# A fused Fourier-filter and ReGLU kernel: another order for its opening, and one copy at its end

## The chip, the core and the metric

One core of one Trainium2 chip runs the whole program. The metric is the device time of one execution in microseconds (us), lower is better. The profile's engines are PE (TensorE: matmuls; PEld is its weight load), DVE (VectorE), ACT (ScalarE), POOL (GpSimd) and SP (SyncE, which here only issues DMAs). Each engine works through its own instructions in program order, and waits at an instruction until its inputs are there and its output buffer is free. DMAs are issued from SP, ACT and POOL; those of POOL are the only ones here that change the type (fp32 in HBM to bf16 on chip).

## The reference

```python
# x: (8, 3008, 256) fp32, filt_r and filt_i: (1505, 256)
X = np.fft.rfft(x, axis=1)
Y = X * (filt_r + 1j * filt_i)[None]
y = np.fft.irfft(Y, n=3008, axis=1).astype(np.float32)
# then a gated feed-forward layer on the 24064 rows of y
gate = np.maximum(y @ w_gate, 0.0)          # w_gate, w_val: 256 x 1536
out = ((gate * (y @ w_val)) @ w_out)        # w_out: 1536 x 256, fp32 out
```

## The kernel before, in words

The transform of length 3008 is split as 94 x 32. A sequence is handled in four stages: a first transform over the 94 rows (matrix `WA`, tiles `psA`, L265), a second one over the 32 columns (`fwd`, `psX`, L402), the product with the filters (`product`, L419 to L422), the inverse of the second transform (`inv`, `psD`, L445), and the inverse of the first (`item_c`, `psY`, L538), which gives 512 rows of y at a time, transposed, in `yT`. The feed-forward layer then runs over 47 blocks of 512 rows (`gv`, L555 to L560; `o_part`, L576 to L600). It is the long loop of the kernel. The stages of the sequences ("batches") 1 to 7 are put into that loop at fixed steps, so that they run amid the matmuls of the layer.

The change touches the opening, ahead of the loop, and the very end.

**The opening.** Batch 0 goes through all stages, and batch 1 through the first one. The order is written out by hand; the scheduler changes nothing of it.

- SP and ACT issue the loads of batch 0's x (`load_x`, L190), SP then the tables. POOL issues the two filters (`load_filters`): each is loaded in four pieces of odd rows (L231, read backwards) and four pieces of even rows (L236). The order is: odd pieces of the real filter, odd of the imaginary, even of the real, even of the imaginary. POOL's DMAs share eight semaphores in turn, so a DMA waits until the one eight before it has landed.
- A one-line DMA on SP, `hold` (L647), reads two rows of the real filter `Ftr` and so waits for its first odd and first even piece. Behind it SP issues batch 1's x, in four quarters of three DMAs each (256 KB per DMA), into the buffers that batch 0's x had.
- PE makes the first transform of batch 0 (`a_0`), ACT copies the tiles out (L277), DVE transposes four quarters (`turn_0`, L300).
- `first_b`: `fwd(0, i)` for i = 0 to 5, each into two PSUM banks (e = 0, 1). For each bank there are two products, k = 0 with the real filter (`tt`) and k = 1 with the imaginary (`uu`). Those of (i, e) = (0, 1), (1, 1), (2, 1) go by way of an ACT copy (`xs`, L419) to POOL (L420), all others are DVE's (L422). `make_back_u` makes a table on ACT (L216, L218) that `inv` needs. `inv(0, q)`, q = 0 to 2, takes the products of i = 2q and 2q + 1, fills four banks, and is copied out to `DS0` (L458). `warm(n)` runs n matmuls on junk (L611).
- Amid this stand the "items": batch 1's first transform in 16 pieces (`a_1`), each one `psA` bank and one ACT copy (L290; half of them in two parts). Items 0 to 3 need the first quarter of batch 1's x, 4 to 7 the second, and so on. When item 13 is done, SP stores a half of the result to HBM and loads it back in another layout.
- After the third inverse, DVE turns `DS0` in two halves of d (`turn_d`, L300), `item_c(0, 0)` and `item_c(0, 1)` make the first `yT`, and the loop starts with its first `psV`.

There are eight PSUM banks. A stage takes the one that was given back longest ago and waits until whoever read it last is done. Before the change two, two and two items stand in `first_b`, then come seven, the two `item_c`, and the last three.

**The end.** The last block's output is copied bank by bank (L589) and stored from three DMA queues (L600). The last of its four tiles is copied in two halves: columns 0 to 127 by DVE (L585), columns 128 to 255 by ACT (L586).

Of the kernel before, what the change touches and what calls it, by code (L numbers as in the profile page):

```python
# [116 lines left out]
def kernel(  # L117
# [18 lines left out]
    W = 512  # L136
# [19 lines left out]
    def done(t):  # L156
        free.append(held.pop(id(t))[0])
# [68 lines left out]
    def load_filters():  # L226

        for src, dst in FILT:
            for c in range(4):
                r, k1, n = 32 * c + 1, 1 + H * c, H - c // 3  # L230
                nc.gpsimd.dma_start(dst[r:r + 31:2, :n, :],  # L231
                                    _ap(src, (N1 - k1) * D, [[N1 * D, 16], [-D, n], [1, D]]))
        for src, dst in FILT:
            for c in range(4):
                r, k1, n = 32 * c, 1 + H * c, H - c // 3
                nc.gpsimd.dma_start(dst[r:r + 31:2, :n, :], _ap(src, k1 * D, [[N1 * D, 16], [1, n * D]]))  # L236
# [31 lines left out]
    def a_0(n2, nn, d0, nd):  # L268

        psA = a_bank(n2, nn, d0, nd)  # L270
        dq = D // 4
        l, q = n2 % NC2, slice(d0 // dq, (d0 + nd) // dq)
        c = n2 // NC2
        dst = AS0.rearrange("p q (l c) e (g f) -> p l c g q e f", c=2, g=2)[:, l:l + nn, c // 2, c % 2]
        src = psA.rearrange("p n (q e f) -> p n q e f", e=dq // 2, f=2)
        for i in range(nd // dq):
            nc.scalar.copy(dst[:, :, q.start + i], src[:, :, i])  # L277
        done(psA)

    def a_1(p, s, h):  # L280
# [21 lines left out]

    def turn_0(q):
        w = D // 8
        turn_pairs(ats[0][:, :, q * w:q * w + w], AS0[:, q])

    def turn_1(i):
        w = D // 8
# [79 lines left out]
    ON_POOL = ((0, 1), (1, 1), (2, 1))  # L388
    ats = {}

    psXs, tus, left, xs = {}, {}, {}, {}
# [43 lines left out]
    def inv(b, q):  # L435
# [3 lines left out]
        for m in range(2):  # L439
            for k in range(last + 1):  # L440
                for r in range(2):
                    for c in range(4):
                        for e in range(2):
# [6 lines left out]
        dst = sb.tile([128, 8, D], BF16, tag="dsb", bufs=3, name="dsb") if b else DS0  # L450
        def out(cs):
            for c in cs:
                copy = nc.vector.tensor_copy if (c % 2 if b else (q, c) in ((1, 3), (2, 0), (2, 1))) else nc.scalar.copy
                if b:
                    copy(dst[:, c:8:4, :], psD[c])
                else:
                    k, g = 4 * q + c // 2, c % 2 * 2
                    copy(dst[:, k:k + 3:2, :, g:g + 2], psD[c].rearrange("p m (f e) -> p m e f", f=2))  # L458
                done(psD[c])
        if not b:  # L460
            return out(range(4))

        def rest():
            out((2, 3))
# [6 lines left out]

    def first_b(item):

        def products(i, es=(1, 0)):
            for e in es:
                for k in range(2):
                    product(0, i, e, k, pool=(i, e) in ON_POOL)

        for i in range(3):
            fwd(0, i)  # L480
            if i < 2:
                products(i)
        make_back_u()
        products(2)
        warm(3)
        fwd(0, 3)
        products(3, (1,))
        warm(3)
        fwd(0, 4)
        item(2)  # L490
        products(3, (0,))
        inv(0, 0)
        fwd(0, 5)
        products(4)
        item(2)
        products(5)
        place_own()
        inv(0, 1)
        item(2)
        inv(0, 2)  # L500

    dCs = {}
# [29 lines left out]
    def item_c(k, h):  # L532

        if h == 0:
            yTs[k] = sb.tile([128, 2, W], BF16, tag="yT", bufs=3, name="yT")
        psY = bank("psY", W)
        for (o, b, n2, n1, w) in runs(k * W, W):
            nc.tensor.matmul(psY[:, o:o + w],  # L538
                             d_rows(b, n2, h),
                             M1[:, 1, n1:n1 + w] if b == 0 else M1[:NROW, 0, n1:n1 + w],  # L540
                             start=True, stop=True)
        dst = yTs[k][:, h]
        if h == 0 or k:
            nc.scalar.copy(dst, psY)  # L544
        else:
            nc.vector.tensor_copy(dst, psY)
        done(psY)


# [18 lines left out]
    def o_part(blk, s, prods):  # L568
# [9 lines left out]
        if s in (5, 11) or last and s % 3 == 2:  # L578
# [2 lines left out]
                osb = XP[t][:, 0:1, :].rearrange("p k (h d) -> p (k h) d", d=D)  # L581
            else:
                osb = fs.tile([128, 2, D], FP32, tag="osb", bufs=4)
            if s == 11 and last:
                nc.vector.tensor_copy(osb[:, 1, 0:D // 2], psO[:, 1, 0:D // 2])  # L585
                nc.scalar.copy(osb[:, 1, D // 2:], psO[:, 1, D // 2:])  # L586
            else:
                copy = nc.vector.tensor_copy if last else nc.scalar.copy
                copy(osb[:, t0 % 2:t % 2 + 1], psO[:, t0 % 2:t % 2 + 1])  # L589
            done(psO)  # L590
            late = last or blk == NB - 2 and s == 11
            for tt in range(t0, t + 1):
# [49 lines left out]
    for r in range(2):  # L642
        make_back_t(r)
        if not r:
            warm(4)
    hold = sb.tile([2, 8], BF16, tag="hold", bufs=1)
    nc.sync.dma_start(hold, Ftr[0:2, 4, 0:8])  # L647
    load_x(1, sp, ((0, 0, 2 * q), (0, 2 * q, 4 * q), (1, 0, 2 * q), (1, 2 * q, 4 * q)))
    items = iter([(p, s, h) for p in range(4) for h in range(2) for s in range(2)])

    def item(n):
# [110 lines left out]
```

## Time and profile before

| What | us |
|---|---|
| Median of 3 runs (866.09 to 868.73) | 868.37 |
| Time of the profiled execution | 865.68 |
| Its span, first to last instruction | 863.80 |
| Granted TensorE clock, mean | 0.999 |
| First matmul of the long loop (`psV`), from the span's start | 45.59 |
| Last matmul of the kernel ends | 858.21 |

The page's busy shares are: PE 98%, PEld 58%, DVE 67%, ACT 57%, POOL 53% of the span. A view of windows gives PE 4.09 us of 5 between 20 and 25 us and 4.59 of 5 between 25 and 30, part of it junk matmuls; it gives 5.00, 5.00 and 4.95 in the three windows of 5 us that follow 35. In the timeline a row gives the start and the time of a run of like instructions, the engine, the line, the operation, the tile written and read, the shape and the count; the bracket at its end says how long the engine had been idle before it and whose event ended that.

### The profile page before, as it was taken

To read this page: it belongs to the slowest core of one execution; us is meant where nothing else is said; L and a number is where in the kernel's file an instruction comes from. 1 tells how busy PE (TensorE), PEld (TensorE's weight loads), DVE (VectorE), ACT (ScalarE), POOL (GpSimd) and SP (SyncE) were. 2 spreads that over 40 slices of the span, in tenths; PEclk is the share of its full clock that TensorE was granted. 3 is DMA by queue.
4 is the path that set the end of the run, shared out by engine and by line. 5 is a ranking of instruction groups with operands and counts; after the bars stand their busy time and mean duration, and the time that the engine had idled before them with its cause. 6 is when DMAs were issued, how large, how long until landed. Compare 5 with 4: busy or idle time off the path is not lost.

```text
span 863.8 us, 20396 instructions
## 1 busy us (share of the span) xinstructions
PE 848.7 (98%) x7587; PEld 498.8 (58%) x7704; DVE 577.8 (67%) x863; ACT 494.6 (57%) x904; POOL 458.4 (53%) x496
## 2 busy tenths in 40 slices
PE   9999999999999999999999999999999999999997
PEld 4456655656556555556556655565655656666665
DVE  3878865777657775577765787658865688555553
ACT  5765565555655556555555555555556555555552
POOL 6747890488986765776666756767450023000001
PEclk9999999999999999999999999999999999999999
DMA  9985365334782339633386333762464422611111
GB/s 250 241 164 122 96 158 138 109 113 110 190 183 88 84 87 192 166 98 98 85 208 142 95 103 100 190 151 74 101 130 108 99 58 52 126 43 29 37 35 52
DMA packets 101366, 101.61 MB, mean 118 GB/s; under 512 B 21827, under 2 KB 89955, under 8 KB 99730
## 3 DMA queue, kind: packets, MB, share of 16 engines
q1 hardware_dynamic: 81986, 77.96, 36.1%
q0 software_dynamic: 18928, 21.82, 11.7%
q8 instruction: 61, 1.00, 0.5%
q10 hardware_dynamic: 352, 0.52, 0.2%
q14 instruction: 39, 0.32, 0.1%
HBM read 58.23 MB, written 45.88 MB: 121 GB/s over the span
## 4 chain that ended last, share of the span: by engine, by line
PE 94%; DMA 2%; issue 1%; DVE 1%; ACT 1%; SPq 1%; POOL 0%; DVEq 0%; ACTq 0%
PE psG L555 29%; PE psO L576 28%; PE psV L555 26%; PE psA L265 3%; PE psF L367 3%; PE psY L538 3%; PE psD L445 2%; PE psX L402 1%; DMA XF<-in_x_dram 1%; DMA Abuf<-asb 1%; ACT vsb L558 1%; DVE prod L560 1%; SPq L190 0%; DVE tt L422 0%; DMA out_dram<-osb 0%
## 5 line engine op out<-in xcount | busy, mean ns | idle before, releaser
L560 DVE SCALAR_TENSOR_TENSOR prod<-psG,vsb 128x512 bf16<-128x512 f32 x564 | 389.4, 691 | 235.8 <-ACT vsb L558 231.6
L558 ACT CAST vsb<-psV 128x512 bf16<-128x512 f32 x564 | 332.2, 589 | 225.8 <-PE psV L555 121.1
L576 PE MATMUL psO<-WoT,prod 128*128 128x256 bf16 x2256 | 336.6, 273 | 0.8
L555 PE MATMUL psG<-yT,WgT 128*128 128x512 bf16 x1111 | 331.8, 379 | 5.2
L555 PE MATMUL psV<-yT,WvT 128*128 128x512 bf16 x1030 | 314.9, 380 | 0.1
L576 PEld LDWEIGHTS <-prod 128*128 128x128 bf16 x2256 | 220.6, 98 | 143.4
L555 PEld LDWEIGHTS <-WgT 128*128 128x128 bf16 x1128 | 110.0, 97 | 133.5
L432 POOL TENSOR_TENSOR pp<-tt,uu 128x256 bf16<-128x256 f32 x84 | 60.9, 725 | 170.7 <-DVE uu L422 162.5
L555 PEld LDWEIGHTS <-WvT 128*128 128x128 bf16 x1128 | 100.3, 98 | 37.3 <-issue 25.6
L544 ACT CAST yT<-psY 128x512 bf16<-128x512 f32 x93 | 54.5, 586 | 43.2 <-PE psY L538 42.6
L589 ACT COPY osb<-psO 128x512 f32<-128x512 f32 x92 | 54.1, 588 | 22.1 <-PE psO L576 20.7
L600 POOL DMA_DIRECT2D out_dram<-osb x5 | 2.6, 534 | 119.6 <-ACT osb L589 118.0
L422 DVE TENSOR_TENSOR tt<-psX,Ftr 128x512 f32<-128x512 f32 (+1 forms) x93 | 63.5, 683 | 0.5 <-PE psX L402 0.5
L422 DVE TENSOR_TENSOR uu<-psX,Fti 128x512 f32<-128x512 f32 (+1 forms) x93 | 63.3, 681 | 0.3 <-DMA Fti<-in_filt_i_dram 0.3
L433 POOL TENSOR_TENSOR pp<-tt,uu 128x256 bf16<-128x256 f32 x84 | 60.9, 726 | 0.0
L353 POOL TENSOR_TENSOR fold<-XF 128x1024 f32<-128x1024 f32 x24 | 56.3, 2347 | 5.8 <-DMA XF<-in_x_dram 5.4
L354 POOL TENSOR_TENSOR XF<-XF 128x1024 f32<-128x1024 f32 x24 | 56.4, 2350 | 1.9
L257 POOL CAST scr<-prod 128x8 f32<-128x8 bf16 x19 | 3.6, 190 | 85.8 <-DVE prod L560 71.7
L340 POOL DMA_DIRECT2D XF<-in_x_dram x76 | 45.6, 602 | 2.0 <-issue 1.3
L374 ACT CAST asb<-psF 128x512 bf16<-128x512 f32 x48 | 25.8, 589 | 34.5 <-PE psF L367 34.5
L374 DVE CAST asb<-psF 128x512 bf16<-128x512 f32 x48 | 30.9, 686 | 18.0 <-PE psF L367 18.0
L538 PE MATMUL psY<-M,dCb 96*128 96x94 bf16 (+19 forms) x604 | 37.9, 200 | 0.0
(71 smaller groups left out, 457.8 us busy)
## 6 DMA issues: line engine op xcount, KB each, us to landing
Dbuf<-dsb SPq DMA_DIRECT2D x84, 128.0 KB
dCb<-Dbuf SPq DMA_DIRECT2D x56, 192.0 KB
XF<-in_x_dram POOLq DMA_DIRECT2D x38, 256.0 KB, 6.7
Abuf<-asb SPq DMA_DIRECT2D x96, 96.0 KB
at<-Abuf SPq DMA_DIRECT2D x24, 384.0 KB
XF<-in_x_dram SPq DMA_DIRECT2D x31, 256.0 KB
XF<-in_x_dram POOLq DMA_DIRECT2D x76, 96.0 KB, 5.1
out_dram<-osb SPq DMA_DIRECT2D x69, 94.0 KB
```

The lines of the kernel that those rows point to most:

```text
L353: tt(t, xp[:, 0:2], xp[:, 2:4], op=ALU.add)
L354: tt(xp[:, 2:4], xp[:, 0:2], xp[:, 2:4], op=ALU.subtract)
L374: copy(asf[:, :, q, :], banks[q])
L422: nc.vector.tensor_tensor(p, psX, filt, op=ALU.mult)
L432: nc.gpsimd.tensor_tensor(p[:, 0], tt[:, 0], uu[:, 1], op=ALU.subtract)
L433: nc.gpsimd.tensor_tensor(p[:, 1], tt[:, 1], uu[:, 0], op=ALU.add)
L538: nc.tensor.matmul(psY[:, o:o + w], d_rows(b, n2, h), M1[:, 1, n1:n1 + w] if b == 0 else M1[:NROW, 0, n1:n1 + w], start=True, stop=True)
L544: nc.scalar.copy(dst, psY)
L555: nc.tensor.matmul(pt[:, :W], w[:, h, ft * 128:(ft + 1) * 128], yt[:, h, :], start=(h == 0), stop=(h == 1))
L558: nc.scalar.copy(vsb, psV[:, :W])
L560: nc.vector.scalar_tensor_tensor(prod, in0=psG[:, :W], scalar=0.0, in1=vsb, op0=ALU.max, op1=ALU.mult)
L576: nc.tensor.matmul(psO[:, t % 2], prods[ft][:, t * 128:(t + 1) * 128], WoT[:, ft, :], start=(ft == 0), stop=(ft == NFT - 1))
```

## The change

- Filters: all eight pieces of the real one first, then all eight of the imaginary one.
- SP now has two `hold` DMAs. The first waits for the real filter's first odd and even pieces; behind it the first quarter of batch 1's x is issued. The second waits for the same pieces of the imaginary filter; behind it come the other three quarters.
- The last `a_0` tile is copied in two halves on ACT, and the last quarter of `turn_0` is transposed in two halves.
- `first_b`: `fwd` 0 to 3 stand together; then the real products, then items and imaginary products in turn. `make_back_u` stands behind the first two items. The two `warm(3)` are gone. Items now stand as 2, 2, 1, 2, 1 in `first_b`, then seven, the two `item_c`, and one.
- The copies out of `inv`: for q = 0 and 1 all four on ACT. For q = 2 by halves of d: the first half two on ACT and two on DVE, then `turn_d(0)`, the second half four on ACT, then `turn_d(1)`.
- `item_c(0, h)`: the left half of `yT` is copied by ACT, the right half by DVE.
- The end: the last tile is copied whole, by DVE.

```diff
@@ load_filters
                 nc.gpsimd.dma_start(dst[r:r + 31:2, :n, :],
                                     _ap(src, (N1 - k1) * D, [[N1 * D, 16], [-D, n], [1, D]]))
-        for src, dst in FILT:
             for c in range(4):
@@ a_0
-            nc.scalar.copy(dst[:, :, q.start + i], src[:, :, i])
+            for e in (slice(0, 16), slice(16, 32)) if (n2, d0) == (24, 3 * dq) else (slice(0, 32),):
+                nc.scalar.copy(dst[:, :, q.start + i, e], src[:, :, i, e])
@@ turn_0
-        turn_pairs(ats[0][:, :, q * w:q * w + w], AS0[:, q])
+        n = 2 if q == 3 else 1
+        for i in range(n):
+            e = slice(i * w // n, (i + 1) * w // n)
+            turn_pairs(ats[0][:, :, q * w + e.start:q * w + e.stop], AS0[:, q, :, e])
@@ inv
+        if not b:
+            w = D // 4
+            for h in range(2) if q == 2 else (0,):
+                for c in range(4):
+                    k, g = 4 * q + c // 2, c % 2 * 2
+                    e = slice(h * w, h * w + w) if q == 2 else slice(0, 2 * w)
+                    copy = nc.vector.tensor_copy if (q, h) == (2, 0) and c > 1 else nc.scalar.copy
+                    copy(DS0[:, k:k + 3:2, e, g:g + 2], psD[c].rearrange("p m (f e) -> p m e f", f=2)[:, :, e])
+                if q == 2:
+                    turn_d(h)
...
-                copy = nc.vector.tensor_copy if (c % 2 if b else (q, c) in ((1, 3), (2, 0), (2, 1))) else nc.scalar.copy
...
@@ first_b
-        for i in range(3):
-            fwd(0, i)
-            if i < 2:
-                products(i)
-        make_back_u()
-        products(2)
-        warm(3)
-        fwd(0, 3)
-        products(3, (1,))
-        warm(3)
-        fwd(0, 4)
-        item(2)
-        products(3, (0,))
-        inv(0, 0)
-        fwd(0, 5)
-        products(4)
-        item(2)
-        products(5)
-        place_own()
-        inv(0, 1)
-        item(2)
-        inv(0, 2)
+        for i in range(4):
+            fwd(0, i)
+        for k in range(2):
+            for i in range(3):
+                product(0, i, 1, k, pool=True)
+        for i in range(3):
+            product(0, i, 0, 0)
+        for e in (1, 0):
+            product(0, 3, e, 0)
+        item(2)
+        for i in range(3):
+            product(0, i, 0, 1)
+        make_back_u()
+        item(2)
+        for e in (1, 0):
+            product(0, 3, e, 1)
+        fwd(0, 4)
+        item(1)
+        inv(0, 0)
+        fwd(0, 5)
+        for i in (4, 5):
+            for e in (1, 0):
+                for k in range(2):
+                    product(0, i, e, k)
+            if i == 4:
+                item(2)
+        place_own()
+        inv(0, 1)
+        item(1)
+        inv(0, 2)
@@ item_c
-        if h == 0 or k:
+        if k:
             nc.scalar.copy(dst, psY)
         else:
-            nc.vector.tensor_copy(dst, psY)
+            nc.scalar.copy(dst[:, :W // 2], psY[:, :W // 2])
+            nc.vector.tensor_copy(dst[:, W // 2:], psY[:, W // 2:])
@@ o_part
-            if s == 11 and last:
-                nc.vector.tensor_copy(osb[:, 1, 0:D // 2], psO[:, 1, 0:D // 2])
-                nc.scalar.copy(osb[:, 1, D // 2:], psO[:, 1, D // 2:])
-            else:
-                copy = nc.vector.tensor_copy if last else nc.scalar.copy
-                copy(osb[:, t0 % 2:t % 2 + 1], psO[:, t0 % 2:t % 2 + 1])
+            copy = nc.vector.tensor_copy if last else nc.scalar.copy
+            copy(osb[:, t0 % 2:t % 2 + 1], psO[:, t0 % 2:t % 2 + 1])
@@ the opening's main line
-    hold = sb.tile([2, 8], BF16, tag="hold", bufs=1)
-    nc.sync.dma_start(hold, Ftr[0:2, 4, 0:8])
-    load_x(1, sp, ((0, 0, 2 * q), (0, 2 * q, 4 * q), (1, 0, 2 * q), (1, 2 * q, 4 * q)))
+    for (src, dst), parts in zip(FILT, (((0, 0, 2 * q),), ((0, 2 * q, 4 * q), (1, 0, 2 * q), (1, 2 * q, 4 * q)))):
+        hold = sb.tile([2, 8], BF16, tag="hold", bufs=2)
+        nc.sync.dma_start(hold, dst[0:2, 4, 0:8])
+        load_x(1, sp, parts)
...
-    for h in range(2):
-        turn_d(h)
     item(7)
     for hh in range(2):
         item_c(0, hh)
-    item(3)
+    item(1)
     turn_1(0)
```

More of the change, by code (lines that the diff above doesn't have):

```diff
@@ L386, in load_at_tiled @@
                               _ap(Abuf[b], rr * N2 * NG * D, [[NG * D, 32], [1, NG * D]]))
-    ON_POOL = ((0, 1), (1, 1), (2, 1))
     ats = {}
@@ L449, in inv @@
                                              tile_position=(32 * c, 64 * e))
-        dst = sb.tile([128, 8, D], BF16, tag="dsb", bufs=3, name="dsb") if b else DS0
+        if not b:
[8 more added lines that the diff above has]
+                    turn_d(h)
+            for c in range(4):
+                done(psD[c])
+            return
+        dst = sb.tile([128, 8, D], BF16, tag="dsb", bufs=3, name="dsb")
         def out(cs):
             for c in cs:
-                copy = nc.vector.tensor_copy if (c % 2 if b else (q, c) in ((1, 3), (2, 0), (2, 1))) else nc.scalar.copy
-                if b:
-                    copy(dst[:, c:8:4, :], psD[c])
-                else:
-                    k, g = 4 * q + c // 2, c % 2 * 2
-                    copy(dst[:, k:k + 3:2, :, g:g + 2], psD[c].rearrange("p m (f e) -> p m e f", f=2))
+                copy = nc.vector.tensor_copy if c % 2 else nc.scalar.copy
+                copy(dst[:, c:8:4, :], psD[c])
                 done(psD[c])
-        if not b:
-            return out(range(4))
         def rest():
@@ L472, in first_b @@
     def first_b(item):
[L474 to L477, printed above, removed]
-        for i in range(3):
-            fwd(0, i)
-            if i < 2:
-                products(i)
-        make_back_u()
-        products(2)
-        warm(3)
-        fwd(0, 3)
-        products(3, (1,))
-        warm(3)
+        for i in range(4):
[3 more added lines that the diff above has]
+                product(0, i, 1, k, pool=True)
+        for i in range(3):
+            product(0, i, 0, 0)
[4 more added lines that the diff above has]
+            product(0, i, 0, 1)
+        make_back_u()
+        item(2)
+        for e in (1, 0):
+            product(0, 3, e, 1)
         fwd(0, 4)
-        item(2)
-        products(3, (0,))
+        item(1)
         inv(0, 0)
         fwd(0, 5)
-        products(4)
-        item(2)
-        products(5)
+        for i in (4, 5):
[4 more added lines that the diff above has]
+                item(2)
         place_own()
         inv(0, 1)
-        item(2)
+        item(1)
         inv(0, 2)
@@ L583, in o_part @@
                 osb = fs.tile([128, 2, D], FP32, tag="osb", bufs=4)
-            if s == 11 and last:
-                nc.vector.tensor_copy(osb[:, 1, 0:D // 2], psO[:, 1, 0:D // 2])
-                nc.scalar.copy(osb[:, 1, D // 2:], psO[:, 1, D // 2:])
-            else:
-                copy = nc.vector.tensor_copy if last else nc.scalar.copy
-                copy(osb[:, t0 % 2:t % 2 + 1], psO[:, t0 % 2:t % 2 + 1])
+            copy = nc.vector.tensor_copy if last else nc.scalar.copy
+            copy(osb[:, t0 % 2:t % 2 + 1], psO[:, t0 % 2:t % 2 + 1])
             done(psO)
```

## The prediction

> **What bounds the kernel now.** The chain of waits comes first. The page gives its shares, and its list in order of time gives the opening:
>
> ```profile
> PE 94%; DMA 2%; issue 1%; DVE 1%; ACT 1%; SPq 1%; POOL 0%; DVEq 0%; ACTq 0%
> ```
> ```profile
> 9.75 10.54 PE psA L265 x24
> ...
> 21.05 0.58 SPq L190
> 21.64 0.05 issue
> 21.69 4.97 DMA XF<-in_x_dram
> 26.66 0.14 issue
> 26.80 1.96 PE psA L265 x4
> ...
> 36.34 6.21 PE psA L265 x14
> 42.54 0.54 PE psY L538 x12
> 43.09 2.67 PE psA L265 x6
> 45.75 0.43 PE psV L555 x2
> ```
>
> From 45.6 us on the chain is matmuls of the long loop, one behind the other. The change does not touch the loop, so it can win or lose only ahead of it and behind it. In the opening the chain leaves PE once, for the first quarter of batch 1's x: PE has nothing to do until it lands at 26.66. The second view is the timeline of PE, for what PE does in that time:
>
> ```profile
> 23.05 0.82 PE L611 MATMUL psJ<-junk 128*128 128x512 bf16 x2
> 23.80 0.42 PE L402 MATMUL psX<-at,F 64*32 64x256 bf16 x15
> 25.20 0.28 PE L402 MATMUL psX<-at,F 64*32 64x256 bf16 x1 [0.98 <-issue]
> 25.42 0.82 PE L611 MATMUL psJ<-junk 128*128 128x512 bf16 x3
> 26.17 0.42 PE L402 MATMUL psX<-at,F 64*32 64x256 bf16 x16
> ```
>
> Between 23.1 and 26.8 only two `fwd` (0.23 each of PE's time) are of use: some 3.2 us of PE are free. Third, the queues of POOL and SP:
>
> ```profile
> 10.29 2.20 POOL L231 DMA_DIRECT2D Ftr<-in_filt_r_dram  x4 [0.33 <-issue]
> 12.46 2.19 POOL L231 DMA_DIRECT2D Fti<-in_filt_i_dram  x4
> 16.16 1.97 POOL L236 DMA_DIRECT2D Ftr<-in_filt_r_dram  x4 [1.51 <-DMA Ftr<-in_filt_r_dram]
> ```
> ```profile
> 19.65 0.75 SPq L647 DMA_DIRECT2D hold<-Ftr  x1
> 20.51 8.65 SPq L190 DMA_DIRECT2D XF<-in_x_dram  x12
> ```
>
> The first filter piece lands at 16.16 (POOL goes on), the ninth at 19.65 (`hold` goes on), the last at 23.67 (the first `uu` on DVE had waited for it). Fourth, the end:
>
> ```profile
> 858.25 0.29 DVE L585 COPY XF<-psO 128x128 f32<-128x128 f32 x1 [0.88 <-PE psO L576]
> 858.92 0.27 ACT L586 COPY XF<-psO 128x128 f32<-128x128 f32 x1 [5.32 <-DMA out_dram<-osb]
> 859.21 0.96 ACTq L600 DMA_DIRECT2D out_dram<-XF  x2
> ```
>
> ACT is issuing DMAs until 858.67, so its half copy starts 0.67 after DVE's, and the last stores wait for it.
>
> **The change, part by part.**
>
> *When the first x quarter lands (call it L).* The even piece that `hold` needs becomes the fifth filter piece instead of the ninth. Pieces land 0.44 apart by (19.65 - 16.16) / 8, or 0.5 by 96 KB at the 190 GB/s of the DMA view between 15 and 18 us; so the fifth lands at 17.65 to 17.9, and I take 17.75, 1.9 earlier. Before, the quarter landed 26.66 - 19.65 = 7.0 after that: 2.84 for `hold` and three issues (to 22.49), and 4.17 of flight. The same gives L = 24.75. The x loads' own rows range from 2.9 us of flight, with a median of 3.5, which give 23.5 and 24.1. I take 24.4, between the median and the old one, for now more filter pieces are still behind it. The upper end is 26.66, as before, if the quarter has to wait for them.
>
> *From L to the loop.* I put each engine's instructions in the new order, each starting when its engine, its inputs and its bank are free, with the durations of the rows. On the path:
> - Item 0 starts at L + 0.14 (26.66 to 26.80); its ACT copy 1.13 later (27.93), item 1's 0.86 after that, 0.58 long: L + 2.7.
> - `make_back_u` is now behind these copies on ACT: 2.0 (23.96 to 25.98), L + 4.65. Behind it wait the copies of items 2 and 3, in pairs of 0.54: L + 5.75. Before, it ran while ACT was idle.
> - The third bank of `inv(0, 0)` is item 3's, so it starts at L + 5.8. It takes 1.1 to the copies, the first copy 0.6: L + 7.5. That bank is item 5's. POOL's last product for this inverse, moved behind three real ones, ends at 29.3 and is needed at L + 6.4 = 30.8.
> - Then on PE: two items 1.9, `inv(0, 1)` 1.0, item 7 1.0, `inv(0, 2)` 1.0: L + 12.45 = 36.85 (before 36.27).
> - Seven items 6.3 (6.14 before, and a wait for copies), `item_c` 0.5. The changed program has DVE's right half of `yT` wait for ACT's left half, so ACT 0.38 and DVE 0.43 follow one another, about 1.25 from the end of `psY` to the loop. Only one item (0.9) hides that, where three did.
>
> That is L + 20.5. The same walk over the old order ends at 45.75 where the trace has 45.59, so I take off 0.16: L + 20.35 = 44.75, against 45.59: -0.85. The ends: L cannot count below 23.6 (the fourth `fwd` and the first `xs` copies are in front), 44.0, -1.6; L = 26.66 gives 47.0, +1.4.
>
> *What lies beside this.* The second x quarter (item 4, ahead of `inv(0, 0)`) waits on SP for the 13th piece. That landed at about 21.5 and now shares with three x DMAs; by the same 7.0, less old contention, it comes at 28.5 to 29.5, and it is needed by L + 4.7 = 29.1: 0 to 0.4, at 0.1 in the sum. The imaginary filter's last piece is late by the 2 us that 768 KB take at 380 GB/s, less the slot won: about 25. DVE has five real products until 25.75, and POOL needs it at 27.0, so this is hidden; each microsecond past 26.5 would push the products. `turn_d`: two ACT halves of 0.27, then two turns of 2.3, end 5.9 after `inv(0, 2)`, under the seven items (6.3); with whole copies they would end 0.7 later and show 0.3. The halves in `a_0` and `turn_0` cost some 0.05 each on ACT and DVE, ahead of the wait for L: 0, and 0.1 without it. The dropped junk matmuls (1.6) were in free time. The weights were issued from 31.2 to 34.1 and landed 6.8 after issue, by 41; cover 3.7. The HBM round trip of item 13's half starts some 2 us sooner, its reader one: 0.
>
> *The end.* DVE copies 128x256 in 0.42 (its earlier copies of L589): done at 858.67 instead of ACT's 859.18, and SP and ACT, both free of issues by then, follow with their last stores. ACT still has 0.2 of semaphores there. So -0.3 to -0.5. POOL's queue, drained at 861.56 against SP's 862.16 (the waits behind the last store), allows up to -0.6; 0 if other stores hold the last ones back. I take -0.45.
>
> *Sum.* -0.85 + 0.1 - 0.45 = -1.2: the span goes from 863.8 to 862.6, the profiled time from 865.7 to 864.5. The median of the runs, 868.37, lies 2.7 above that execution; against it, 867.2.
>
> **The rivals.**
>
> *The quarter lands early.* Small filter pieces (odd rows) may yield to large x packets; then L is under 23.6, and POOL and ACT set the pace: -1.6 - 0.55 = -2.15, 866.2. For it: small pieces got nothing through between 12 and 13.8 us while x was flowing (issued at 10.29, first landing 16.16). Against: the even pieces come into the same stretch.
>
> *Slower: x waits behind the filters.* POOL now issues imaginary pieces without a gap, so their rings are full when x comes. If the quarter lands at 26.66 as before, everything above hangs on it, because `make_back_u` stands behind items 0 and 1 on ACT, where before ACT, DVE and `fwd` went on without x. The loop then starts at 47.0: +1.4 - 0.45 = +0.95, 869.3. With the end's gain it decides from L = 25.7 on (45.59 + 0.45 - 20.35). Against: before, x came to run beside the last pieces and pieces were still on time by 23.67. The Trainium skill (DMA: Bandwidth & Descriptors, Queues, rings and completion order) has each DMA engine take turns between its queues, so that neither would wait for the other's whole backlog; no view of this run shows the turns.
>
> *The clock.* PE's free time now has no junk in it: from 23.6 to L, and 1.4 us ahead of `inv(0, 0)`. The trace has a hole of 0.98 in this stretch, at a granted clock of 1.00. If the clock were halved after a hole, items 0 to 3 (3.6 us) would take twice as long: 867.2 + 3.6 = 870.8. The Trainium skill (TensorE: Matmul & The Clock Gate, What's actually happening) says that the clock halves after an idle window of about 3.4 us. By that rule this comes only with L above 27; the trace's hole, shorter, agrees.
>
> *The front's gain is given back.* If batch 1's round trip or the weights set the loop's first steps, only the end's gain is left: 867.9. Against: the old loop shows no such wait, with later data.
>
> **How the numbers follow.** Chances: forecast 0.44 (its own range, L from 23.8 to 25.2: 865.9 to 868.2 with half a microsecond of spread), early 0.26, behind the filters 0.18, clock 0.04, given back 0.08. The old runs spread over 2.6 us, which is 0.3%, about what a measurement of this kernel can tell from no change. The early case lies 0.45 inside that bound, so half of it would read faster, of the forecast three in ten: 0.27. Slower: the clock, a quarter of the late case and a remainder, 0.10. The range takes in the early and the late case with a spread of 1.2 below, less above: 865.0 to 869.3.
>
> **What would show it.** L in the chain: the first item on PE at 24.5 instead of 26.8, then `make_back_u` behind its copies on ACT, `inv(0, 0)` at 30.2 waiting for an ACT copy, `turn_d` done before the seventh item, the first `psV` near 44.8, and DVE's last copy of 0.42 with both stores right behind it. It is wrong if x lands after 25.7, if PE waits for `turn_d` or for DVE's products, if the granted clock falls, or if the loop itself changes its length of 812.6 us.

## The result, and the profile after

| What | before | after |
|---|---|---|
| Median of 22 runs each, same chip (us) | 866.99 (865.61 to 869.74) | 869.67 (867.20 to 871.41) |
| Ratio of the times, with 95% interval | | 1.0027 (1.0017 to 1.0036) |
| Span of the profiled execution | 863.8 | 867.4 |
| First matmul of the long loop, from the span's start | 45.59 | 49.31 |
| Length of the loop, to the last matmul's end | 812.62 | 812.71 |
| Last matmul's end to the span's end | 5.6 | 5.4 |

The kernel became slower by 0.27%. The forecast was 867.2 with faster ahead of slower. The two profiled executions differ by 3.6 us: the loop starts 3.72 later, keeps its length (+0.09), and the end is 0.24 shorter. So in these two executions all of the loss lies ahead of the loop. (Two executions of the experiments ran far slower than all others, the profiled one of e5 at 1493.79 us and one of e8 at 1795.67; no ratio counts them, and e5 therefore has no loop start.)

The chain of waits of the changed kernel, first its shares, then its list in order of time (start, length, what the chain stands on):

```profile
PE 96%; DMA 2%; SPq 1%; POOL 1%; issue 0%; ACT 0%; POOLq 0%
```
```profile
12.64 5.41 DMA Ftr<-in_filt_r_dram
18.07 0.75 SPq L657
...
20.10 6.91 DMA XF<-in_x_dram
27.01 0.14 issue
27.14 6.36 PE psA L264 x8
...
41.64 6.21 PE psA L264 x14
47.84 0.48 PE psY L550 x12
...
49.31 0.71 PE psV L568 x2
```

The chain still leaves PE for the first quarter of batch 1's x. SP is released at 18.07, 1.6 earlier than before, but the quarter lands at 27.01, where it landed at 26.66. The flight of its last DMA has grown from 4.97 to 6.91. And the eight matmuls of items 0 to 3 behind it take 6.36 us; in both kernels a pair takes 0.9 in the later row of 14 (6.21 / 7).

The timeline of PE around this, and the windows of 2 us (busy time of PE, PEld, DVE, ACT and POOL, then the granted clock, the DMA share and GB/s):

```profile
22.43 1.34 PE L404 MATMUL psX<-at,F 64*32 64x256 bf16 x64
27.14 6.36 PE L264 MATMUL psA<-XF,WA 128*128 128x512 f32 x8 [3.37 <-DMA XF<-in_x_dram]
```
```profile
24.00:26.00 2.00, 0.00 (x0) 0.00 (x0) 1.99 (x4) 0.77 (x2) 2.00 (x2) 0.94 0.87 244
26.00:28.00 2.00, 0.86 (x1) 0.50 (x2) 1.02 (x2) 0.00 (x0) 2.00 (x3) 0.50 0.90 315
28.00:30.00 2.00, 2.00 (x4) 0.84 (x3) 2.00 (x4) 0.59 (x1) 2.00 (x3) 0.50 0.92 279
...
32.00:34.00 2.00, 2.00 (x20) 0.63 (x19) 0.07 (x1) 2.00 (x5) 0.48 (x2) 0.86 0.57 238
```

The free time of PE is now one hole of 3.37 us, and the clock is at one half from its later part until 0.9 us before the eighth matmul ends (33.50). With 1.00 and 0.50 as the only values, 0.94 in a window of 2 us is 0.24 us at a half, so the clock fell at about 25.76, and 0.86 puts its return at about 32.56: 6.8 us.

Why x came no earlier is in the timeline of SP and in the view of DMAs. That view has two lines for each stretch: a queue, its packets, MB and share. q0 carries the filters (POOL), q1 the x loads (SP). The first pair is the stretch from 20.1 to 21.5, the second that from 21.5 to 23.0:

```profile
18.07 0.75 SPq L657 DMA_DIRECT2D hold<-Ftr  x1
18.92 1.76 SPq L190 DMA_DIRECT2D XF<-in_x_dram  x3
23.62 0.63 SPq L657 DMA_DIRECT2D hold<-Fti  x1
24.36 5.62 SPq L190 DMA_DIRECT2D XF<-in_x_dram  x9
```
```profile
q0 software_dynamic: 269, 0.19, 113.4%
q1 hardware_dynamic: 6, 0.04, 7.4%
...
q1 hardware_dynamic: 54, 0.32, 55.9%
q0 software_dynamic: 62, 0.13, 47.2%
```

The three x DMAs (768 KB) were issued from 18.92 to 20.68. Until 21.5 they moved 0.04 MB, while filter pieces moved 0.19 MB in the last 1.4 us of that alone. Some 2.5 us after its first issue x had moved 0.26 MB in the kernel before (20.51 to 23.0); here it was 0.04. x then shared with the remaining pieces until 25. The issue came earlier into a stretch in which the filters had the DMA engines.

The walk from the landing to the loop, on ACT and DVE, and the end of the kernel:

```profile
30.93 0.59 ACT L290 CAST dCb<-psA 128x512 bf16<-128x512 f32 x1 [1.12 <-PE psA L264]
31.42 0.20 ACT L216 CAST conj<-tabs 128x2 f32<-128x2 bf16 x1
31.64 1.76 ACT L218 ACTIVATE I2u<-I2t,conj 128x768 bf16<-128x768 bf16 x2
33.31 1.17 ACT L290 CAST asb<-psA 128x256 bf16<-128x256 f32 x4
```
```profile
26.98 3.08 DVE L424 TENSOR_TENSOR uu<-psX,Fti 128x512 bf16<-128x512 f32 x5 [0.99 <-issue]
42.79 4.51 DVE L300 STREAM_TRANSPOSE dCb<-AS 128x2048 f32<-128x2048 f32 x2 [0.28 <-ACT AS L459]
48.84 0.76 DVE L559 CAST yT<-psY 128x256 bf16<-128x256 f32 x2 [1.54 <-ACT yT L558]
```
```profile
859.95 3.59 ACTq L609 DMA_DIRECT2D out_dram<-XF  x7
861.88 1.03 POOL L609 DMA_DIRECT2D out_dram<-XF  x2
862.07 0.42 DVE L598 COPY XF<-psO 128x256 f32<-128x256 f32 x1 [0.88 <-DMA out_dram<-osb]
```

`make_back_u` (L216, L218) stands behind two item copies, as foreseen, 31.42 to 33.40. `turn_d` ends at 47.30, ahead of `psY` (47.84). DVE's halves of `yT` start behind ACT's, and the loop follows 0.99 after the end of `psY` (48.32 by the chain). DVE's last copy takes 0.42 with no ACT copy behind it.

### The profile page after: what moved, and what is told of

The parts are those of the page before. It is cut to its first block, busy times and chain, and to the rows that moved or that the text cites. A ratio compares the mean times of both kernels' runs of the same rounds, so it can differ in the third digit from the quotient of the medians.

```text
span 867.4 us, 20514 instructions
## 1 busy us (share of the span) xinstructions
PE 856.0 (99%) x7698; PEld 499.6 (58%) x7698; DVE 576.5 (66%) x864; ACT 495.6 (57%) x910; POOL 459.2 (53%) x496
## 4 chain that ended last, share of the span: by engine, by line
PE 96%; DMA 2%; SPq 1%; POOL 1%; issue 0%; ACT 0%; POOLq 0%
PE psV L568 29%; PE psG L568 28%; PE psO L589 28%; PE psF L370 3%; PE psY L550 3%; PE psA L264 2%; PE psD L447 2%; PE psX L404 1%; DMA XF<-in_x_dram 1%; DMA Ftr<-in_filt_r_dram 1%; SPq L190 1%; POOL out_dram L609 0%; POOL Ftr L231 0%; SPq L657 0%; ACT osb L598 0%
## 5 line engine op out<-in xcount | busy, mean ns | idle before, releaser
L568 PE MATMUL psV<-yT,WvT 128*128 128x512 bf16 x1128 | 336.1, 379 | 0.0
L568 PE MATMUL psG<-yT,WgT 128*128 128x512 bf16 x1128 | 335.3, 379 | 0.0
L568 PEld LDWEIGHTS <-WvT 128*128 128x128 bf16 x1128 | 100.3, 98 | 37.5 <-issue 25.8
L377 ACT CAST asb<-psF 128x512 bf16<-128x512 f32 x48 | 25.8, 589 | 34.5 <-PE psF L370 34.5
```

What stands on the lines that cost most here:

```text
L377: copy(asf[:, :, q, :], banks[q])
L568: nc.tensor.matmul(pt[:, :W], w[:, h, ft * 128:(ft + 1) * 128], yt[:, h, :], start=(h == 0), stop=(h == 1))
```

## The experiments

Two theories came out of this. *Clock*: the hole without junk halves the granted clock, and that is most of the 3.7 us. *Order*: the new order behind the landing (`make_back_u`, halves, fewer items as cover) costs it, whatever the clock does. Beside both stood the loads: without the late x neither would show. Ratios are to the kernel before on the same chip, with 95% intervals; "loop" is the first `psV` of the profiled execution (45.59 before, 49.31 after).

**e1: junk in the hole.** The changed kernel with 14 junk matmuls ahead of the first item:

```diff
             product(0, 3, e, 0)
+        warm(14)
         item(2)
```

> The changed kernel with 14 junk matmuls (128x512) put between the fourth fwd and the first item, so that PE is busy until the x quarter lands. Theory (late quarter and halved clock): the quarter still lands at about 27.0, the granted clock stays at 1.00, eight rows of items 0 to 3 take 3.6 us instead of 6.36, and the loop starts near 27.0 + 20.35 = 47.4 instead of 49.3; ratio to the kernel before about 1.0015 instead of 1.0027. Rival (the order of work on ACT sets the pace and the clock costs nothing of its own): the loop starts at 49.3 again, ratio 1.0027.

Measured: 871.92, ratio 1.0067 (1.0048 to 1.0086); loop at 53.09. A miss. In PE's timeline:

```profile
23.52 0.59 PE L621 MATMUL psJ<-junk 128*128 128x512 bf16 x2
27.76 4.45 PE L621 MATMUL psJ<-junk 128*128 128x512 bf16 x12 [3.65 <-issue]
32.05 3.60 PE L264 MATMUL psA<-XF,WA 128*128 128x512 f32 x8
```

After two of the junk matmuls PE stood for 3.65 us with nothing in the trace that it waited for; the view of DMAs shows an instruction packet on queue 8 in this stretch. The junk then ran late, from 27.76 to 32.21 and mostly at half clock (0.50 from 28.2 to 31.6), in front of the items. Of x's first quarter the trace has the last piece there at 28.15, so the items could have started some 3.8 us sooner than 32.05. The run doesn't judge the theory. What it shows is that PE can stand in this stretch for another reason than x (the last section has the likely one).

**e2: x ahead of the filters' holds.** The first quarter is issued with no hold, the rest behind one on `Fti`:

```diff
-    for (src, dst), parts in zip(FILT, (((0, 0, 2 * q),), ((0, 2 * q, 4 * q), (1, 0, 2 * q), (1, 2 * q, 4 * q)))):
-        hold = sb.tile([2, 8], BF16, tag="hold", bufs=2)
-        nc.sync.dma_start(hold, dst[0:2, 4, 0:8])
-        load_x(1, sp, parts)
+    load_x(1, sp, ((0, 0, 2 * q),))
+    hold = sb.tile([2, 8], BF16, tag="hold", bufs=2)
+    nc.sync.dma_start(hold, Fti[0:2, 4, 0:8])
+    load_x(1, sp, ((0, 2 * q, 4 * q), (1, 0, 2 * q), (1, 2 * q, 4 * q)))
```

> The changed kernel with the first x quarter issued ahead of the first hold, so that it no longer waits for any filter; one hold, on the imaginary filter, stays for the other three. Theory: the quarter is there before the fourth fwd ends, PE has no hole over 1.5 us, the clock stays at 1.00, the loop starts near 44.0 and the time is 1.5 to 2.2 us under the kernel before (ratio 0.9975 to 0.998). The imaginary filter ends at about 25, still ahead of its first use. Rival (the new order of products and items is itself the loss): the loop starts later than 45.6 although the quarter is early, ratio over 1.0.

Measured: 868.92, ratio 1.0021 (1.0009 to 1.0033), with runs from 866.01 to 871.15. The profiled execution is the fastest of them, so the trace is of a good case: loop at 45.99, clock 1.00. PE's timeline there:

```profile
23.74 4.05 PE L264 MATMUL psA<-XF,WA 128*128 128x512 f32 x8
...
30.49 1.10 PE L264 MATMUL psA<-XF,WA 128*128 128x512 f32 x2 [2.34 <-DVE uu L424]
```

With x there in time the hole ahead of the first items, and the halved clock with it, is gone in this execution. But item 4 then starts at 30.49, and since the second quarter's hold went on at 24.57 only, that quarter is what it had to wait for: its last piece landed at 30.24, while the releaser named, DVE's `uu`, had been done since about 27.4. What the first quarter gains the second gives back. The other runs are not all like this one: in six of the eleven the mean clock is 0.995 to 0.997, against 0.999 here, so there it must have fallen (their median is 869.67, that of the other five 868.08).

**e3: the end alone.** The kernel before, with only the last copy changed:

```diff
-            if s == 11 and last:
-                nc.vector.tensor_copy(osb[:, 1, 0:D // 2], psO[:, 1, 0:D // 2])
-                nc.scalar.copy(osb[:, 1, D // 2:], psO[:, 1, D // 2:])
-            else:
...
+            copy = nc.vector.tensor_copy if last else nc.scalar.copy
```

> The kernel before with only the last output copy changed to one whole copy on DVE. Theory: 0.2 to 0.5 us less between the last matmul and the end, ratio 0.9994 to 0.9998, not to be told from 1. Rival (the tail loses): more than 5.6 us from the start of the last DVE copy to the end.

Measured: 866.73, ratio 1.0009 (0.9998 to 1.0020). From the start of DVE's last copy to the end are 5.28 us against 5.57, a gain of 0.3 in the trace, too small for the runs.

**e4: the old loads.** The changed kernel with the loads of before (odd and even pieces in the old order, one hold):

```diff
+        for src, dst in FILT:
             for c in range(4):
...
+    hold = sb.tile([2, 8], BF16, tag="hold", bufs=2)
+    nc.sync.dma_start(hold, Ftr[0:2, 4, 0:8])
+    load_x(1, sp, ((0, 0, 2 * q), (0, 2 * q, 4 * q), (1, 0, 2 * q), (1, 2 * q, 4 * q)))
```

> The changed kernel with the loads of the kernel before: filter pieces in the old order, one hold on the real filter, all of batch 1's x behind it. Theory: the quarter lands at 26.5 to 27 as in both kernels, PE has a hole of about 3 us without junk, and the loop starts between 47.0 (clock held) and 49.3 (clock halved); ratio 1.001 to 1.0027. Rival (the new order of the loads is the loss): the loop starts at 45.6 or earlier, ratio at most 1.0.

Measured: 869.70, ratio 1.0035 (1.0023 to 1.0047), loop at 49.57. PE's timeline:

```profile
27.10 6.66 PE L265 MATMUL psA<-XF,WA 128*128 128x512 f32 x8 [2.72 <-DMA XF<-in_x_dram]
```

The quarter lands at 26.96 with the old loads too, and the new order of the work, with no matmul between 24.4 and 27.1, loses as much as the whole change. The clock is 0.50 from 26.3 to 33.1. So the new loads alone aren't the loss.

**e5 to e8: fewer, longer junk matmuls; `make_back_u` early; both.** In e6 `make_back_u()` stands ahead of the first items. In e5 four fp32 junk matmuls (each as long as an item's) fill the hole; e7 has both. e8 is e2 with `make_back_u` early and item 4 behind `inv(0, 0)`. In e5 and e7 (and in e10 and e11 below) the 18 short junk matmuls at the kernel's start are also nine of twice the length. Only the parts that matter are shown.

```diff
+        make_back_u()                 # e6, e7, e8
         for i in range(3):
             product(0, i, 0, 0)
...
+        junk32(4)                     # e5, e7: matmuls on XF[1], into one bank
         item(2)
...
-        make_back_u()                 # e6, e7, e8
...
         fwd(0, 4)
-        item(1)                       # e8
         inv(0, 0)
+        item(1)                       # e8
         fwd(0, 5)
```

> The changed kernel with four fp32 junk matmuls (0.88 us each) between the fourth fwd and the first item, and with the 18 opening junk matmuls of 256 columns made 9 of 512, so that PE's instruction count up to here is not larger. Theory (the halved clock is a cost of its own): PE is busy from 23.7 to about 27, the quarter still lands near 27, the clock stays at 1.00, items 0 to 3 take 3.6 us instead of 6.36, the loop starts near 47.4 instead of 49.3; ratio to the kernel before 1.001 to 1.002. Rival (a PE that waits for its instructions, as the fourteen junk matmuls of the earlier run did at 24.1): a hole without a releaser follows the junk, and the clock falls again.

> The changed kernel with make_back_u moved back ahead of the first two items, so that ACT runs it while PE waits for x. Theory: at the halved clock the items are slower (1.7 us each) than ACT's copies, so the inverse waits for PE and this alone brings 0 to 0.5 us: loop start 48.8 to 49.3, ratio 1.0022 to 1.0035. Rival (the place of make_back_u sets the pace): 1.2 to 1.5 us sooner, loop start near 48, ratio about 1.0015.

> Both edits of the two runs above together. Theory: with the clock held ACT is the bound, and make_back_u now costs nothing: loop start near 27.0 + 19.2 = 46.2, ratio 0.9995 to 1.0015. Rival (the two do not add): loop start as with the junk alone.

> The changed kernel with the first x quarter issued ahead of the holds, make_back_u ahead of the items, and item 4, which needs the second quarter, moved behind the first inverse. Theory: PE goes from the fourth fwd straight into items 0 to 3, waits at most 1.5 us for POOL's products ahead of the first inverse, the clock stays at 1.00, and the loop starts at 43.9 to 44.7; 0.9 to 2 us less than the kernel before, ratio 0.9977 to 0.999. Rival (the imaginary filter, late by the x quarter, sets the pace): the loop starts at 45.6 or later.

| | median | ratio | loop |
|---|---|---|---|
| e5 | 881.50 | 1.0166 (1.0153 to 1.0179) | - |
| e6 | 868.93 | 1.0034 (1.0022 to 1.0046) | 48.77 |
| e7 | 881.39 | 1.0163 (1.0148 to 1.0177) | 60.55 |
| e8 | 866.69 | 1.0008 (0.9996 to 1.0020) | 45.58 |

e5 and e7 missed by a fault of the edit: the junk read a buffer of batch 1's x, and so waited for its last quarter. PE's timeline of e7:

```profile
34.57 6.74 PE L621 MATMUL psJ<-XF,WA 128*128 128x512 f32 x8 [11.28 <-DMA XF<-in_x_dram]
```

It says something all the same: with the hole made 11.28 long the clock was at 0.50 from 27.1 to 40.8, through the junk itself. e6's hole is 3.82 and its clock falls too, but for 3.4 us only:

```profile
27.59 5.37 PE L264 MATMUL psA<-XF,WA 128*128 128x512 f32 x8 [3.82 <-DMA XF<-in_x_dram]
```

From here to its loop e6 takes 21.18 us, 0.99 less than the changed kernel (27.14 to 49.31). Its first eight item matmuls alone take 0.99 less (5.37 against 6.36), so the shorter fall of the clock accounts for all of it, and the earlier `make_back_u` shows no gain in this trace, nor in the runs (1.0034 against 1.0027). e8 holds the clock at 1.00 in its trace and is back at the time of before. Its item 4 still waits for the second quarter: that landed at 31.22, and the item starts at 31.47.

**e9: the old junk taken out of the kernel before.** Both `warm(3)` are left out:

```diff
-        warm(3)
         fwd(0, 3)
         products(3, (1,))
-        warm(3)
```

> The kernel before without its two warm(3). It leaves out junk work only. Theory: the two fwd between keep PE's holes under 1.5 us, the clock stays at 1.00 in most executions, loop start 45.5 to 45.8, ratio 0.9995 to 1.0005. Rival (the junk is what holds the clock in the kernel before): the clock falls to 0.50 ahead of the first items and the loop starts 1 to 2 us later, ratio 1.001 to 1.003.

Measured: 867.83, ratio 1.0001 (0.9987 to 1.0015), with runs from 864.98 to 869.88. In the profiled execution the loop starts at 48.03, and the clock is 0.50 from 25.8 to 32.6. PE's timeline:

```profile
24.59 0.70 PE L402 MATMUL psX<-at,F 64*32 64x256 bf16 x15 [0.72 <-DVE uu L422]
...
26.48 3.75 PE L265 MATMUL psA<-XF,WA 128*128 128x512 f32 x4 [1.19 <-ACT xs L419]
```

Here the clock fell with `fwd` work in between and no hole above 1.2 us; the first two items take 3.75 instead of 1.96. The trace bears out that junk matters. So do the clocks of the runs: their mean is 0.997 or less in 9 of these 12, against 6 of 29 of the kernel before on the same chip (a fall of 6.8 us takes 0.004 off the mean). The times don't show it clearly: the ratio's interval reaches from 0.9987 to 1.0015.

**e10, e11: junk on a tile of its own.** The junk of e5 reads a tile that nothing else writes (four fp32 matmuls, 3.7 us); e11 has `make_back_u` early as well:

```diff
+    wide = pro.tile([128, 512], FP32, tag="wide", bufs=1)
...
+    def junk32(n):
...
+        psJ = bank("psJ", 512)
+        for i in range(n):
+            nc.tensor.matmul(psJ, WA, wide, start=True, stop=True)
+        done(psJ)
...
+    nc.vector.memset(wide, 0.0)
...
+        make_back_u()                 # e11
         for i in range(3):
             product(0, i, 0, 0)
...
+        junk32(4)
         item(2)
```

> The changed kernel with four fp32 junk matmuls (0.88 us each) between the fourth fwd and the first item, on a tile of their own that no DMA writes, and with the 18 opening junk matmuls of 256 columns made 9 of 512, so that PE's instruction count up to here is not larger. Theory (the halved clock is a cost of its own): PE is busy from 23.7 to about 27, the quarter lands near 27 as before, the clock stays at 1.00, items 0 to 3 take 3.6 us instead of 6.36, the loop starts near 47.3 instead of 49.3; ratio to the kernel before 1.001 to 1.002 instead of 1.0027. Rival (ACT sets the pace, the clock costs nothing of its own): loop start 49 or later.

> The kernel of the run above with make_back_u moved ahead of the first two items. Theory: with the clock held ACT is the bound from the quarter's landing on, so this brings 0.7 to 1.1 us more: loop start 46.2 to 46.6, ratio 1.000 to 1.0015. Rival: no difference to the run above.

Measured: e10 867.89, ratio 1.0016 (1.0004 to 1.0029), loop at 48.34; e11 868.09, ratio 1.0008 (0.9996 to 1.0020), loop at 47.59. PE's timeline of e10, then of e11:

```profile
23.37 3.70 PE L622 MATMUL psJ<-wide,WA 128*128 128x512 f32 x8
28.36 3.67 PE L264 MATMUL psA<-XF,WA 128*128 128x512 f32 x8 [1.29 <-DMA XF<-in_x_dram]
...
48.34 0.71 PE L569 MATMUL psV<-yT,WvT 128*128 128x512 bf16 x2
```
```profile
28.11 3.67 PE L264 MATMUL psA<-XF,WA 128*128 128x512 f32 x8 [0.28 <-DMA XF<-in_x_dram]
33.12 0.42 PE L447 MATMUL psD<-tt,I2t 32*64 32x256 bf16 x16
```

The clock is 1.00 in every window from 22 to 36 in both. e10's windows around the hole, to be laid beside those of the changed kernel:

```profile
24.00:26.00 2.00, 2.00 (x6) 0.86 (x5) 1.52 (x3) 0.30 (x1) 2.00 (x3) 1.00 0.79 227
26.00:28.00 2.00, 1.07 (x3) 0.19 (x1) 0.00 (x0) 0.00 (x0) 0.78 (x1) 1.00 0.66 191
28.00:30.00 2.00, 1.64 (x4) 0.87 (x5) 1.90 (x4) 0.51 (x1) 1.88 (x2) 1.00 0.98 340
```

Although x lands 1.2 later than in the changed kernel (28.23), the loop starts 1.0 earlier. From the first item to the loop it takes 22.17 in the changed kernel, 19.98 in e10 and 19.48 in e11: in these traces the clock is worth 2.2 us, and the place of `make_back_u`, with the clock held, 0.5. e6 against e11 gives a check of the first: both have `make_back_u` early, and e6, whose clock was at a half for 3.4 us, takes 1.70 longer to the loop (21.18), all of it in its first items (5.37 against 3.67). That the junk holds the clock is borne out by the runs: the mean clock is 0.997 or less in 2 of the 23 runs of e10 and e11, and in 19 of the 22 of the changed kernel. What it gains in time the runs alone show for e11 only just, and not for e10, whose interval overlaps that of the changed kernel (1.0017 to 1.0036).

**e12: the new loads alone**, in the kernel before (odd and even pieces of one filter together, two holds):

```diff
-        for src, dst in FILT:
             for c in range(4):
...
-    hold = sb.tile([2, 8], BF16, tag="hold", bufs=1)
-    nc.sync.dma_start(hold, Ftr[0:2, 4, 0:8])
-    load_x(1, sp, ((0, 0, 2 * q), (0, 2 * q, 4 * q), (1, 0, 2 * q), (1, 2 * q, 4 * q)))
+    for (src, dst), parts in zip(FILT, (((0, 0, 2 * q),), ((0, 2 * q, 4 * q), (1, 0, 2 * q), (1, 2 * q, 4 * q)))):
+        hold = sb.tile([2, 8], BF16, tag="hold", bufs=2)
+        nc.sync.dma_start(hold, dst[0:2, 4, 0:8])
+        load_x(1, sp, parts)
```

> The kernel before with only the loads of the change: the real filter first, two holds, the first x quarter amid the filters. Theory (the quarter queues behind filter pieces that are already in the rings, so the earlier issue wins nothing): the hold goes on near 18, the quarter lands at 27.0 to 28.2, not earlier than the 26.66 of the kernel before; the imaginary filter lands near 27 instead of 23.7, and DVE, which takes both products of a bank in turn here, is late by 3 us: loop start 47 to 48.5, ratio 1.002 to 1.0035. Rival (the loads win and the new order of the work loses it): the quarter lands at 25 or sooner.

Measured: 869.62, ratio 1.0036 (1.0023 to 1.0050), loop at 49.06. DVE's and PE's timelines:

```profile
26.61 0.69 DVE L421 TENSOR_TENSOR uu<-psX,Fti 128x512 bf16<-128x512 f32 x1 [3.60 <-DMA Fti<-in_filt_i_dram]
```
```profile
26.15 0.28 PE L401 MATMUL psX<-at,F 64*32 64x256 bf16 x1 [2.33 <-issue]
```

The old order of work wants the imaginary filter early. It is there at 26.6 only, and DVE's products wait 3.60 for it. PE stands twice: 2.33 us before 26.15, with no releaser in the trace (on this too see the last section), and 0.93 behind those products at 27.36. The first items start at 29.11, and the clock halves for one stretch of 3.4 us. The new loads alone don't bring x earlier either: SP was released at 18.21, and the quarter's last piece landed at 26.64, as in the kernel before (26.66). Either half of the change alone thus costs as much as both (e4, e12), by another road to the same hole.

**e13: x first, a short hold, `make_back_u` early.** As e2 and e6, but the hold reads one row of an odd piece of `Fti`:

```diff
-    hold = sb.tile([2, 8], BF16, tag="hold", bufs=2)
-    nc.sync.dma_start(hold, Fti[0:2, 4, 0:8])
+    hold = sb.tile([1, 8], BF16, tag="hold", bufs=2)
+    nc.sync.dma_start(hold, Fti[1:2, 4, 0:8])
```

> The changed kernel with the first x quarter ahead of the holds, make_back_u ahead of the items, and the hold for the other three quarters on one row of the imaginary filter's odd piece alone, so that it goes on some 2 to 3 us sooner than at 25.5. Theory: item 4 waits less for the second quarter (31.5 in the run that had it behind the first inverse), PE has no hole over 1.5 us, loop start 44.3 to 45.3, ratio 0.998 to 0.9997. Rival (whatever x gains the filter loses on the same DMA engines): loop start 45.6 or later, ratio 1.000 or more.

Measured: 866.69, ratio 0.9999 (0.9987 to 1.0010), runs from 864.52 to 868.96; loop at 44.51 in the profiled (fastest) execution, 1.1 ahead of before. PE's timeline:

```profile
24.25 2.92 PE L264 MATMUL psA<-XF,WA 128*128 128x512 f32 x6
27.57 1.13 PE L264 MATMUL psA<-XF,WA 128*128 128x512 f32 x2 [0.41 <-ACT dCb L290]
...
29.00 1.10 PE L264 MATMUL psA<-XF,WA 128*128 128x512 f32 x2
```

No hole, no wait at item 4, clock 1.00. It is the best form of this order that was found, the equal of the kernel before and not shown to beat it. Among its runs the time goes with the clock: four with a mean of 0.996 or 0.997 took 867.1 to 869.0 us, seven with 0.998 or more took 864.5 to 866.8.

**e14: the rest of the change.** Loads, `first_b` and places of items as before; what stays of the change are the copies, the halves and the end. Against the changed kernel, with the loads as in e4:

```diff
...
         for i in range(3):
-            product(0, i, 0, 1)
+            fwd(0, i)
+            if i < 2:
+                products(i)
         make_back_u()
-        item(2)
...
+        products(2)
+        warm(3)
+        fwd(0, 3)
+        products(3, (1,))
+        warm(3)
         fwd(0, 4)
-        item(1)
+        item(2)
...
     for hh in range(2):
         item_c(0, hh)
-    item(1)
+    item(3)
```

> The changed kernel with the loads, the first_b and the items of the kernel before: what is left of the change is the copies and transposes by halves and the last copy on DVE. Theory: these lie under PE's work, loop start 45.4 to 45.9 with the quarter at 26.7, 0.2 less at the end, ratio 0.999 to 1.0005. Rival (the serial halves of yT or the ACT copies of the inverse cost something): loop start 46 or later.

Measured: 867.13, ratio 1.0006 (0.9996 to 1.0016). These parts neither cost nor win anything that the runs can tell. (Its profiled execution starts the loop at 47.88, with the clock at 0.50 from 27.9 to 31.3; so a trace with the old order can have it as well.)

## Why the prediction was wrong

**Where x lands: the step that failed.** "I take 24.4, between the median and the old one, for now more filter pieces are still behind it." The release of SP was right (17.75 foretold, 18.07 measured). The flight wasn't: 6.3 us from the last of the three issues (20.68) to 27.01, where before it was 4.17. The rows of 2.9 to 3.5 us that pulled the estimate down are of transfers with little beside them. The measured 27.01 lies even behind the "upper end" of the step, 26.66, and the rival "x waits behind the filters" had its argument right: the filters still had the DMA engines when x came. The Trainium skill's rule that was set against this rival (DMA: Bandwidth & Descriptors, Queues, rings and completion order: each engine takes turns between queues) fits from 21.5 on, when both queues move, 0.32 and 0.13 MB in 1.5 us; from 20.1 to 21.5, with 0.04 MB of x against 0.19 of filters, the trace doesn't show such turns.

**The clock: the rival that was right in kind and given too little.** It had 0.04, since it was to come "only with L above 27". L came at 27.01, so this chance hung on the step above, and a late x should have carried it along. The place was right (items 0 to 3) and the price too high: 3.6 foretold, 2.2 by e10 against after (and 1.7 for a fall of half that length, by e6 against e11). The items themselves lost 2.7 (6.36 against 3.67); the rest was hidden. The bound was also too strict: the clock fell with a hole of 2.72 (e4) and with none above 1.2 (e9).

**From the landing to the loop: right.** The walk gave 20.35, of which 20.2 from the first item on. With the clock held it is 19.98 (e10). Of the excess over the kernel before (18.79), `make_back_u` is 0.5 (e11). Of the other 0.7, about 0.35 is `fwd(0, 4)`, which before stood ahead of the first item (26.17) and now stands behind it (33.44 to 33.79 in the changed kernel). The rest is mostly that items stand alone: one takes 1.05 to 1.06 in e11, against 0.96 in a pair, and the last one ahead of the loop 1.13, against 0.89 in a row. So the two halves of `yT` one behind the other, to which the prediction gave part of this, have at most some 0.2 left. This split is worked out from rows; no run has the halves of `yT` alone.

**The sum.** In the traces: items start 0.34 later (27.14 against 26.80), clock 2.2, `make_back_u` 0.5, `fwd(0, 4)` and the single items 0.7: 3.7, the whole delay of the loop. Against the loop start that was forecast, 44.75, it is 4.56 late: 2.61 from the landing (27.01 for 24.4) and 2.2 from the clock, less some 0.2 in the walk. The prediction accepted a slower walk (1.4 with its own numbers, 20.2 less 18.8) as the price of 2.26 won on x, and those 2.26 didn't come. The medians differ by 2.7, not 3.6: runs of the kernel before have clocks from 0.996 to 1.000, and those of the changed one 0.994 to 0.998, so some runs of before seem to lose a part of it too (e9 and e14 show how). Nor does all of the spread lie in the opening. e3's profiled execution starts its loop at 46.27, 0.7 behind that of before, but its span is 3.2 longer (867.0); in its loop PE waits 2.3 us for a round trip through HBM, a wait that the loop of before doesn't have (`psX` behind the load of `at` from `Abuf`).

**Beside this.** Right: `turn_d` under the items, weights and round trip without a wait, the loop's length, junk in free time as far as its own duration goes. What was missed about the junk is that it held the clock. The imaginary filter was thought to be in by 25, and DVE's first `uu` started at 26.98 with 0.99 of waiting; x was later still, so it cost nothing here. `inv(0, 0)` didn't wait for ACT, as items at half clock were slower than the copies.

**The end: right in kind, mis-sized.** The term was -0.45; after has -0.24, e3 -0.3.

**What stays open**: why the landing of x varies from 27.0 to 28.2 between kernels with equal loads (after, e6, e11, e10). A DMA lands in sixteen pieces, and in e6 and e10 fifteen of the quarter's last sixteen are there by 25.70 and 26.50, and one comes 1.7 us later (27.45, 28.23); what held that one is not shown. Open is also why in kernels with the old order the clock is kept in some executions and lost in others (a likely reason stands at the end). With a spread of some 4 us in the runs, that decides more than most edits of the opening.

## What to carry to other kernels

An earlier issue buys an earlier landing only if the DMA engines are free: count the bytes of each queue in the stretch into which the transfer is moved, not the flight times of quiet ones. Before work or junk is taken out of a stretch in which PE waits, price the clock behind it: at one half the first two items took 3.75 us instead of 1.96 in e9, and one late transfer then costs its delay and that. A new order that is slower by design and repaid by one earlier transfer has a single point of failure, which deserves the larger part of the doubt.

## What was not expected of the hardware

- The granted clock needs less than a full idle stretch to fall. Its fall, read from the windows, was at 25.76 in the changed kernel, 2 us into the hole; at 26.28 in e4, 1.9 us into a hole of 2.72; at 28.31 in e6, 0.7 after a hole of 3.82; at 25.83 in e9, with matmuls between. It lasted 6.8 us (after, e4, e9) or 3.4 (e6, e12, e14). The Trainium skill (TensorE: Matmul & The Clock Gate, What's actually happening) has two rates and a free-running window of about 3.4 us; rates and lengths agree with it. With that length laid back from each fall, PE was busy for 1.4 us of it in the changed kernel, 1.5 in e4, 0.7 in e6 and 2.1 in e9, which disagrees with the page's "after ≥1 idle window". Laid forward, it is one length where PE was busy throughout (e6, e12), and two where idle time was left in the first (1.4 us after, 0.8 in e4, 0.65 in e9). The traces record the clock more finely than the views of 2 us, and there each stretch of one value is a whole number of 3.413 us: after has six at 1.00 from 5.26, then two at 0.50. Where these lie differs between executions (the first at 1.00 begins 3.97 to 6.62 us after the span's start), so the same hole can fall into one of them or across two. e2's hole of 2.34 us lies across a boundary at 29.36: PE was busy for 2.19 of the 3.41 us on one side and 2.28 on the other, and the clock held. Busy time alone doesn't draw the line, though. The clock fell after stretches with 2.07 (e9) and 2.13 us (e14) and held after 2.19 (e2) and 2.35 (before), but it held after 1.91 as well (e8). Which matmuls count is open, and that the place of the windows makes the scatter of e9 and e14 is argued, not shown.
- PE can stand with no releaser in a stretch in which the DMA engines are loaded: 3.65 us in e1, 2.33 in e12, 0.98 in the kernel before. Holes of this kind, 0.49 to 3.65 us long, are in six traces (before, e1, e3, e8, e12, e14), and in each the matmul behind the hole is PE's 449th to 451st matmul or weight load; a second one in e1 (0.87 at 45.77) comes 512 later. In each of the six a packet of 16 KB on queue 8, which carries instructions, had ended 1.3 to 1.5 us before PE went on (23.67 and 25.20 in the kernel before, 26.29 and 27.76 in e1, 24.73 and 26.15 in e12). All six fit PE waiting there for its instructions, and the traces show nothing else that it waited for. In e1 and e12 the packet started late (25.21 and 23.65, against 22.78 before); that the data on the loaded DMA engines held it up is likely, and no run shows it.
